# A down product in fp16 terms in place of fp32r: three fp16 copies of each weight tile, scaled by a bound from norms

## The chip, the core and the metric

The kernel runs on one core of one Trainium2 chip. Its time is device microseconds of one execution, the median of several. The engines have short names in the profile: PE is the matrix engine (TensorE) and PEld its weight load, DVE is VectorE, ACT is ScalarE, POOL is GpSimd, and SP issues the DMAs.

## What is computed

The input x has 2048 rows of 576. Two branches read it and are mixed row by row by a gate g:

```python
g = _sigmoid((x * gate_w).sum(-1, keepdims=True))
a = _A_ref(x, A_wq, A_wk, A_wv, A_wo, A_beta)   # attention with memory, 32 heads, 4 segments of 512
b = _B_ref(x, B_w_gate, B_w_up, B_w_down)       # (silu(x @ w_gate) * (x @ w_up)) @ w_down
return g * a + (1 - g) * b
```

The change touches the last product of the second branch, with `w_down` of 4608 x 576: the **down product**. All inputs are fp32, and the kernel keeps nearly fp32's precision by splitting each operand into a high and a low term and adding three products: high by high, high by low, low by high.

## The kernel before, in words

**Stages.** Up to 235 us of the profile the kernel projects x to q, k, v and updates the memory, segment by segment (`qk`, `v_step`, `mem_step`). In between it takes sums of squares or greatest squares of x and of the first weights (`square` on ACT, `peak` on DVE) into columns of a small tile `sc`, 128 columns of one fp32 per partition. From them come powers of two as scales: `sx` for x, `sw[i]` for the weights of four tiles f (i = f // 4); `power` sums a column across partitions by a matmul with ones (L141) and rounds by integer operations on the bits (L142 to L146); `back` makes the inverse `iw[i]` (L149, L150).

**The feed-forward loop** goes over 2 halves of the rows (1024 each) and 36 tiles f of 128 hidden columns. For one f, seven products of a fast scheme (`seven`, a function called with j = 0 to 6; each is seven f16 matmuls of 512 columns, six on L1304 and the last on L1307) make gate and up sums in three PSUM banks `a`, `y`, `xx`, with copies on ACT and additions on DVE between them (L1381, L1384, L1388, L1391, L1395, L1396). Two Silus (L1398, L1400, each with the scale `iw`) and two products on DVE (L1406, L1407) give `sg0` and `sg1`, the hidden rows. ACT copies them into `hh` and DVE subtracts to get `hl`, both fp32r: `split_by` (L1188, L1189) one or two steps later, or `split` (L124, L125) in the third f of a chunk.

**Chunks and steps.** Three f's make a chunk (CH = 3; q = f % 3 is 0, 1, 2). When the next chunk starts, its first f carries the down product of the chunk before: 16 **groups** (8 blocks of 128 rows by 2 column halves of 320 and 256 of the 576), each of 9 matmuls (3 f's by 3 terms) into one bank (`down_part`, L1089), and `down_end` adds the bank to `ya` on DVE (L1098; L1096 copies for the first chunk). Each f has eight steps (`tick`, k = 0 to 7), called between the products. `beat` in a step first runs what `defer(n, ...)` queued for it n steps ago, then groups (SHARE gives 2, 2, 3, 3, 3, 3 for steps 2 to 7 of the first f) and steps of the attention (`att`). In the first half attention steps run only in steps that have groups; in the second half also elsewhere. So the order on each engine is fixed by the program, and each engine runs its own list in that order. Attention contributes matmuls on L846, L957, L985, L987, exponentials on ACT (L961), maxima on DVE (L864), casts on DVE (L1056) and subtractions on POOL (L1058), in three rotating banks (`ts_tile`).

**Weights, first half only.** `w_make` makes f16 operands of gate and up for the next f: sums on POOL (L318), high parts on ACT (L322), low parts on DVE (L326), stored for the second half, which loads them (`w_fetch`). `d_load` brings a tile of `w_down` (L266), `d_split` makes its high part on ACT (L1070, scaled by `iw`) and the low part on DVE (L1071), and the pair, `dw`, is stored to `dc` (L1072); the second half loads it back (`d_fetch`, L1077). `glance` loads weights and squares them on ACT (L132) in the first f of seven chunks, for `sw[i]` of i = 2 to 8; the sum, `power` and `back` follow in the second f. At f = 24, 27, 30 and 33 `x_second` makes the second half's operands of x (L1232, L1239, L1242). Between the halves, the last chunk's 16 groups run without products beside them. In the tail the output projection (L172) runs with the second half's last 16 groups.

## Time and profile before

| | us |
|---|---|
| median of 3 runs | 1751.36 (1747.77 to 1753.06) |
| profiled execution | 1750.37 |
| its span in the profile | 1748.7 |
| projections, to the first feed-forward product | 0 to 235 |
| first half, f = 0 to 35 | 235 to 910 |
| second half with the groups between the halves | 910 to 1657 |
| tail | 1657 to 1749 |

A group line of the profile reads: line, engine, operation, output and inputs by name, shape and count, then busy time, mean ns of one, then the engine's idle time before them and who ended it. In a timeline the columns are start, length, engine, line, operation; consecutive equal instructions are merged into one row with a count. In the view of one line or tile the three numbers are shortest, median and longest ns. In the view by windows each engine has its busy time and its number of instructions. Matmuls overlap in time, so the length of one is not what it costs.

### The profile page before, as it was taken

The page shows a single profiled execution, that of the slowest core. Times are in us where ns is not written, and L with a number is a line of the kernel's source. Part 1 is how long each engine was busy: PE and PEld are TensorE (multiplying, and loading weights), DVE is VectorE, ACT ScalarE, POOL GpSimd, SP SyncE. Part 2 cuts the span into 40 slices and gives each one's busy share as a digit, 9 for nine tenths or more (in the row PEclk, how much of TensorE's full clock was granted, in tenths as well). Part 3 has the DMA queues.
Part 4 walks back from the last instruction along what each step waited for, and adds up shares of the span by engine and source line. Part 5 has one row for each costly group of instructions (what it writes and reads, how often), then busy time and mean ns, then how long its engine had stood idle before and what let it go on. Part 6 is the DMA issues. An engine that isn't in the chain of part 4 may idle for free.

```text
span 1748.7 us, 34878 instructions
## 1 busy us (share of the span) xinstructions
PE 1714.6 (98%) x12241; PEld 1217.6 (70%) x12241; DVE 1326.4 (76%) x3239; ACT 1024.4 (59%) x1800; POOL 841.7 (48%) x1065
## 2 busy tenths in 40 slices
PE   9999999999999999999999999999999999999999
PEld 7889856666766676567656757766756766776699
DVE  6677676788878888888886877778778777775455
ACT  6756575767676666655754565566456466455411
POOL 3325552255545554665542764555546565553121
PEclk9999999999999999999999999999999999999999
DMA  8656776776687666545554477587577569654544
GB/s 284 224 211 225 237 244 206 224 234 191 179 247 225 205 186 193 185 142 153 169 165 150 123 181 182 132 207 170 125 185 196 143 147 210 167 125 129 184 137 139
DMA packets 341667, 321.89 MB, mean 184 GB/s; under 512 B 193396, under 2 KB 258676, under 8 KB 341492
## 3 DMA queue, kind: packets, MB, share of 16 engines
q1 hardware_dynamic: 341492, 319.67, 63.1%
q8 instruction: 96, 1.57, 0.4%
q14 instruction: 79, 0.65, 0.1%
HBM read 188.51 MB, written 104.86 MB: 168 GB/s over the span
## 4 chain that ended last, share of the span: by engine, by line
PE 79%; DVE 7%; ACT 5%; DMA 3%; issue 3%; SPq 2%; POOL 1%; DVEq 0%; ACTq 0%; POOLq 0%
PE bank L1304 33%; PE bank L1089 23%; PE bank L172 7%; PE bank L1307 5%; PE bank L846 4%; PE bank L957 2%; PE bank L985 2%; PE bank L987 1%; DMA stw<-q 1%; PE bank L919 1%; ACT L1297 1%; DVE xo L1242 1%; PE bank L460 1%; ACT L1398 1%; DMA wo__21835<-wc 0%
## 5 line engine op out<-in xcount | busy, mean ns | idle before, releaser
L1089 PE MATMUL bank<-dw,hh 128*128 128x320 f32 (+1 forms) x2304 | 510.0, 314 | 9.2 <-DVE ya L1098 7.0
L1089 PEld LDWEIGHTS bank<-dw,hh 128*128 128x128 f32 x2304 | 380.3, 190 | 35.0 <-DVE ya L1098 11.1
L1089 PE MATMUL bank<-dw,hl 128*128 128x320 f32 (+1 forms) x1152 | 341.0, 296 | 0.6 <-DVE hl L125 0.5
L1058 POOL TENSOR_TENSOR p<-pe,p 128x512 f16<-128x512 f32 x220 | 273.5, 1243 | 88.1 <-DVE p L1056 60.6
L961 ACT ACTIVATE pe<-bank 128x512 f32<-128x512 f32 x220 | 130.8, 594 | 222.3 <-PE bank L957 197.6
L1098 DVE TENSOR_TENSOR ya<-bank,ya 128x320 f32<-128x320 f32 x352 | 157.5, 453 | 90.1 <-PE bank L1089 87.2
L1089 PEld LDWEIGHTS bank<-dw,hl 128*128 128x128 f32 x1152 | 218.4, 190 | 1.1 <-DVE hl L125 1.1
L1307 PE MATMUL bank<-xr,rh 128*128 128x512 f16 x504 | 191.0, 379 | 0.0
L969 POOL TENSOR_SCALAR_AFFINE_SELECT pe<-pe 128x256 f32<-128x256 f32 (+1 forms) x220 | 92.4, 420 | 188.5 <-ACT pe L961 184.6
L864 DVE CUSTOM_DVE_ANT_0 junk<-bank,cm 128x128 bf16<-128x128 f32 (+2 forms) x352 | 169.8, 483 | 15.0 <-PE bank L846 10.0
L318 POOL TENSOR_TENSOR ws<-raw 128x256 f32<-128x256 f32 x72 | 67.5, 938 | 153.2 <-DMA raw<-in_wf_dram 91.3
L846 PE MATMUL bank<-kst,qst 108*128 108x512 bf16 (+3 forms) x512 | 125.2, 300 | 5.4 <-ACT pe L961 2.1
L1189 DVE TENSOR_TENSOR hl<-row,hh 128x512 fp32r<-128x512 f32 x120 | 110.9, 924 | 16.3 <-ACT hh L1188 16.1
L1056 DVE CAST p<-pe 128x512 f16<-128x512 f32 x220 | 108.2, 492 | 0.1
L1391 ACT ACTIVATE row<-bank 128x512 f32<-128x512 f32 x72 | 43.1, 598 | 106.8 <-PE bank L1307 106.6
L957 PE MATMUL bank<-qst,kst 111*128 111x512 bf16 (+3 forms) x352 | 104.2, 303 | 0.0
L1396 DVE TENSOR_TENSOR row<-bank,row 128x512 f32<-128x512 f32 x72 | 49.7, 691 | 70.7 <-ACT bank L1395 70.3
L172 PE MATMUL bank<-xo,qhi 128*128 128x512 f32 x288 | 91.9, 399 | 0.6 <-DVE xo L125 0.5
L1307 PEld LDWEIGHTS <-rh 128*128 128x128 f16 x504 | 49.3, 98 | 59.5
L1395 ACT ACTIVATE bank<-bank 128x512 f32<-128x512 f32 x72 | 41.9, 582 | 83.1 <-PE bank L1307 81.2
L416 POOL TENSOR_TENSOR q<-qr,q 128x512 bf16<-128x512 f32 x36 | 47.1, 1308 | 82.7 <-ACT q L415 70.2
L903 POOL TENSOR_TENSOR xo<-xr,xo 128x512 f16<-128x512 f32 x60 | 71.0, 1184 | 21.7 <-DVE xo L902 12.4
(1067 smaller groups left out, 4121.8 us busy)
## 6 DMA issues: line engine op xcount, KB each, us to landing
xo<-in_wf_dram SPq DMA_DIRECT2D x65, 320.0 KB
dc<-dw SPq DMA_DIRECT2D x36, 576.0 KB
dw<-dc SPq DMA_DIRECT2D x36, 576.0 KB
raw<-in_wf_dram SPq DMA_DIRECT2D x72, 256.0 KB
rh<-rc SPq DMA_DIRECT2D x72, 168.0 KB
draw<-in_wd_dram SPq DMA_DIRECT2D x36, 288.0 KB
xo<-in_xT_dram SPq DMA_DIRECT2D x33, 256.0 KB
vd<-vps SPq DMA_DIRECT2D x8, 912.0 KB
```

Of the source, the lines that this page charges most:

```text
L172: nc.tensor.matmul(t, st[n], mv[n], start=(n == 0), stop=(n == 13))
L846: nc.tensor.matmul(t[:, c:c + w], qs[:KR, pr, P * i:P * i + P], ks[:KR, pr, 0:w], start=True, stop=True)
L864: nc.vector.tensor_tensor_reduce(junk.bitcast(BF)[:, :w], t[:, c:c + w], cm[:, L - w:L], 1.0, -3.0e38, OP.add, OP.max, m[:, k:k + 1])
L957: nc.tensor.matmul(t[:, c:c + w], ks[:KR + 3, pr, P * j:P * j + P], qs[:KR + 3, pr, P * j:L], start=True, stop=True)
L961: nc.scalar.activation(pe, t, AF.Exp, scale=SCALE)
L1056: nc.vector.tensor_copy(p1, pe)
L1058: nc.gpsimd.tensor_sub(p2, pe, p1)
L1089: nc.tensor.matmul(t, p, q[:, cs], start=(f == CH * c and n == 0), stop=(f == CH * c + CH - 1 and n == 2))
L1098: nc.vector.tensor_add(ya[:, i, cs], t, ya[:, i, cs])
L1189: defer(k + 1, lambda: nc.vector.tensor_sub(lo, src, f32(hi)))
L1304: nc.tensor.matmul(t, w[:, p, z], x[z][:, q], start=first and n == 0, stop=False, skip_group_check=True)
L1307: nc.tensor.matmul(t, rem[:, RPOS[j]], XR[j], start=False, stop=True, skip_group_check=True)
```

## The change

The down product's operands become fp16.

- **Weights.** `dw` holds three fp16 copies instead of two fp32r: the high part, the low part, and the high part divided by 2^11 (STEP). The first two are scaled by a column made in `d_scale`; the third is one more DVE operation. The store to `dc` comes a step later and moves 432 KB for 576.
- **Hidden rows.** The two products on DVE take a third factor, the column `hk[i]`; `hh` is 2^-11 of the result in fp16, `hl` the rest at full size (2^11 larger), so the third product is `hl` by the third copy. Both are half as large in memory.
- **Scales.** `weigh(i)` takes the place of the sum, `power` and `back`: one sum across partitions of the 8 or 9 columns, then 17 (19 for i < 2) small DVE operations that also give `hk`, `ha`, `hb`. `reach` makes a bound of x in the projections, and two squares there move from ACT to DVE. `d_look` squares each weight tile on ACT with a sum; `d_scale` turns three such sums into one scale per chunk, with one or two multiplications on POOL.
- **Places.** All three loads of a chunk's `w_down` stand in steps 0, 1, 2 of its first f (three buffers), the looks in steps 4, 5, 6, `d_scale` in step 0 of the second f; the splits stay where they were. `weigh` stands in step 2 of the third f, where the sum stood in step 1 and the rest in steps 5 and 6 of the second.
- **Results.** `down_end` multiplies the bank by the column `inv[c]` as it adds it to `ya`.

The core of the diff:

```diff
+FLOOR = 1e-10
+STEP = 2.0 ** 11
...
-    dc = dram.tile([FT, P, 2 * D], F32, name="dc")
+    dc = dram.tile([FT, P, 3 * D], F16, name="dc")
...
     sc = consts.tile([P, 128], F32, name="sc")
-    junk = consts.tile([P, L], F16, name="junk")
-    one, sx = sc[:, ONE:ONE + 1], sc[:, SX:SX + 1]
+    junk = consts.tile([P, D], F16, name="junk")
+
+    def column(k):
+        return sc[:, k:k + 1]
+
+    one, sx, xq = column(ONE), column(SX), column(19)
+    hk, ha, hb = ([column(20 + 9 * i + j) for i in range(FT // 4)] for j in range(3))
+    inv = [column(23 + 9 * c) for c in range(9)] + [column(16 + c) for c in range(3)]
     sw = [sc[:, SW + i:SW + i + 1] for i in range(FT // 4)]
...
     def peak(src, c, dst=None):
-        nc.vector.tensor_tensor_reduce(src if dst is None else dst, src, src, 1.0, 0.0, OP.mult, OP.max, sc[:, c:c + 1])
+        nc.vector.tensor_tensor_reduce(src if dst is None else dst[:, :src.shape[1]], src, src, 1.0, 0.0, OP.mult, OP.max, sc[:, c:c + 1])
 
...
 
-    def power(out, t):
-        nc.tensor.matmul(t, one.to_broadcast([P, P]), out, start=True, stop=True)
-        nc.vector.tensor_scalar_max(out, t, 1e-24)
+    def grade(out, t, low=FLOOR):
+        nc.vector.tensor_scalar_max(out, t, low)
         bits = out.bitcast(I32)
...
         nc.vector.tensor_single_scalar(bits, bits, 23, OP.logical_shift_left)
+
+    def across(t, src):
+        nc.tensor.matmul(t, one.to_broadcast([P, P]), src, start=True, stop=True)
+
+    def power(out, t):
+        across(t, out)
+        grade(out, t)
         nc.vector.tensor_scalar_mul(out, out, TOP)
 
-    def back(i):
+    def reach(t):
+        across(t, sc[:, 0:4 * NT])
+        nc.vector.tensor_reduce(sc[:, 0:4], t.rearrange("p (s k) -> p s k", k=NT), axis=AX.X, op=OP.add)
+        nc.vector.tensor_reduce(xq, sc[:, 0:4], axis=AX.X, op=OP.max)
+        nc.vector.tensor_scalar(xq, xq, sx, sx, op0=OP.mult, op1=OP.mult)
+        nc.vector.tensor_mul(xq, xq, xq)
+
+    def weigh(i, t):
+        c = 20 + 9 * i
+        n = 9 if i < 2 else 8
+        e, z, m = sc[:, 0:8], column(8), sc[:, 9:13]
+        across(t[:, :n], sc[:, c:c + n])
+        nc.vector.tensor_reduce(sw[i], t[:, :n], axis=AX.X, op=OP.add)
+        grade(sw[i], sw[i])
+        nc.vector.tensor_scalar_mul(sw[i], sw[i], TOP)
+        nc.vector.tensor_scalar(e, t[:, 0:8], sw[i], sw[i], op0=OP.mult, op1=OP.mult)
+        if i < 2:
+            nc.vector.tensor_scalar(z, t[:, 8:9], sw[i], sw[i], op0=OP.mult, op1=OP.mult)
+            nc.vector.tensor_scalar_add(e, e, z)
+        v = e.rearrange("p (f u) -> p f u", u=2)
+        nc.vector.tensor_mul(m, v[:, :, 0], v[:, :, 1])
+        nc.vector.tensor_reduce(z, m, axis=AX.X, op=OP.max)
+        nc.vector.tensor_mul(z, z, xq)
+        grade(z, z, 2.0 ** 26)
         nc.vector.tensor_mul(iw[i], sw[i], sx)
+        nc.vector.tensor_scalar(hk[i], z, 4.0 * STEP * TOP, iw[i], op0=OP.mult, op1=OP.mult)
+        nc.vector.tensor_scalar(ha[i], hk[i], iw[i], 1.0 / STEP, op0=OP.mult, op1=OP.mult)
+        nc.vector.reciprocal(hb[i], ha[i])
         nc.vector.reciprocal(iw[i], iw[i])
...
     def d_load(f):
-        r = fp.tile([P, D], F32, name="draw", bufs=2)
+        r = fp.tile([P, D], F32, name="draw", bufs=3)
         nc.sync.dma_start(r, wd[f])
...
             z = GAUGE.get(t, ())
-            return [lambda m=m, fn=(square if k == 2 else peak): gauge(m, fn) for k, m in enumerate(z)]
+            return [lambda m=m, fn=(square if k == 2 and m > 9 else peak): gauge(m, fn) for k, m in enumerate(z)]
 
...
                 if s == 2:
-                    if n == 4:
-                        mid.append(lambda: total(sw[1], 29, 38))
                     if n == 6:
-                        mid.append(lambda: power(sw[1], lone_tile([P, 1])))
-                        mid.append(lambda: back(1))
+                        mid.append(lambda: weigh(1, lone_tile([P, 9])))
                     if n == 0:
...
                         power(sx, lone_tile([P, 1]))
-                    if n == 2:
-                        total(sw[0], 20, 29)
+                    if n == 4:
+                        reach(lone_tile([P, 4 * NT]))
                     if n == 6:
-                        power(sw[0], lone_tile([P, 1]))
-                        back(0)
+                        weigh(0, lone_tile([P, 9]))
                 if s:
...
         def d_tile():
-            return fp.tile([P, 2, D], F32R, name="dw")
+            return fp.tile([P, 3, D], F16, name="dw")
+
+        def d_look(f):
+            nc.scalar.activation(junk, draw[f], AF.Square, accum_out=column(123 + f % CH))
+
+        def d_scale(c):
+            t, r = ts_tile([P, CH]), sc[:, 13:16]
+            across(t, sc[:, 123:126])
+            grade(r, t)
+            nc.vector.tensor_scalar_mul(r, r, TOP)
+            fs = range(CH * c, CH * c + CH)
+            at = sorted({f // 4 for f in fs})
+            for i in at:
+                z = [f % CH for f in fs if f // 4 == i]
+                z = r[:, z[0]:z[-1] + 1]
+                nc.vector.tensor_scalar(z, z, ha[i], 2.0 ** 100, op0=OP.mult, op1=OP.min)
+            nc.vector.tensor_reduce(inv[c], r, axis=AX.X, op=OP.min)
+            for n, i in enumerate(at):
+                nc.gpsimd.tensor_mul(column(121 + n), inv[c], hb[i])
+            nc.vector.reciprocal(inv[c], inv[c])
 
...
             d = d_tile()
-            k = iw[f // 4]
+            k = column(121 + f // 4 - f // CH * CH // 4)
             defer(1, lambda: nc.scalar.activation(d[:, 0], r, AF.Copy, scale=k))
-            defer(2, lambda: nc.vector.scalar_tensor_tensor(d[:, 1], r, k, f32(d[:, 0]), op0=OP.mult, op1=OP.subtract))
-            defer(3, lambda: nc.sync.dma_start(dc[f], f32(d).rearrange("p a n -> p (a n)")))
+            defer(2, lambda: nc.vector.scalar_tensor_tensor(d[:, 1], r, k, d[:, 0], op0=OP.mult, op1=OP.subtract))
+            defer(3, lambda: nc.vector.tensor_scalar_mul(d[:, 2], d[:, 0], 1.0 / STEP))
+            defer(4, lambda: nc.sync.dma_start(dc[f], d.rearrange("p a n -> p (a n)")))
             return d
...
             d = d_tile()
-            nc.sync.dma_start(f32(d).rearrange("p a n -> p (a n)"), dc[f])
+            nc.sync.dma_start(d.rearrange("p a n -> p (a n)"), dc[f])
             return d
...
                 d = ws[half, f]
-                dh, dl = d[:, 0], d[:, 1]
-                for n, (p, q) in enumerate(((hh, dh), (hh, dl), (hl, dh))):
-                    nc.tensor.matmul(t, p, q[:, cs], start=(f == CH * c and n == 0), stop=(f == CH * c + CH - 1 and n == 2))
+                for n, (p, q) in enumerate(((hh, 0), (hh, 1), (hl, 2))):
+                    nc.tensor.matmul(t, p, d[:, q, cs], start=(f == CH * c and n == 0), stop=(f == CH * c + CH - 1 and n == 2))
 
...
             if c == 0:
-                nc.vector.tensor_copy(ya[:, i, cs], t)
+                nc.vector.tensor_scalar_mul(ya[:, i, cs], t, inv[c])
             else:
-                nc.vector.tensor_add(ya[:, i, cs], t, ya[:, i, cs])
+                nc.vector.scalar_tensor_tensor(ya[:, i, cs], t, inv[c], ya[:, i, cs], op0=OP.mult, op1=OP.add)
             if c == FT // CH - 1 and hf and half == 0:
...
 
-        def split_by(k, hi, lo, src):
-            defer(k, lambda: nc.scalar.activation(hi, src, AF.Copy))
-            defer(k + 1, lambda: nc.vector.tensor_sub(lo, src, f32(hi)))
+        def h_high(hi, src):
+            nc.scalar.activation(hi, src, AF.Copy, scale=1.0 / STEP)
+
+        def h_low(hi, lo, src):
+            nc.vector.scalar_tensor_tensor(lo, hi, -STEP, src, op0=OP.mult, op1=OP.add)
+
+        def split_by(k, hi, lo, src, lag=1):
+            defer(k, lambda: h_high(hi, src))
+            defer(k + lag, lambda: h_low(hi, lo, src))
 
...
                 plan += [z for z in looked if z[0] >= 0]
-            if half == 0 and pos % 3 == 1 and 2 <= i < FT // 4:
-                plan += [(1, lambda i=i: total(sw[i], 20 + 9 * i, 28 + 9 * i)),
-                         (5, lambda i=i: power(sw[i], ts_tile([P, 1]))), (6, lambda i=i: back(i))]
+            if half == 0 and pos % 3 == 2 and 2 <= i < FT // 4:
+                plan.append((2, lambda i=i: weigh(i, ts_tile([P, 8]))))
             if pos == 24:
...
                 if half == 0:
-                    if (q, k) in ((0, 1), (1, 0), (1, 5)):
-                        g = f + (q == 1 and k == 5)
-                        draw[g] = d_load(g)
+                    if q == 0 and k < CH:
+                        draw[f + k] = d_load(f + k)
+                    if q == 0 and 4 <= k < 4 + CH:
+                        d_look(f + k - 4)
+                    if q == 1 and k == 0:
+                        d_scale(f // CH)
                     if (q, k) in ((1, 1), (1, 7), (2, 5)):
...
             ops, rem = wops.pop((half, f)), rhs[f % 2]
-            hh = fp.tile([P, 2, L], F32R, name="hh")
-            hl = fp.tile([P, 2, L], F32R, name="hl")
+            hh = fp.tile([P, 2, L], F16, name="hh")
+            hl = fp.tile([P, 2, L], F16, name="hl")
             hs[half, f] = hh, hl
...
             seven(xx, 6, False)
-            nc.vector.tensor_mul(sg0, xx, sg0)
-            nc.vector.tensor_mul(sg1, p5, sg1)
-            if q == CH - 1:
-                defer(2, lambda t=(hh[:, 0], hl[:, 0], sg0): split(*t))
-            else:
-                split_by(2, hh[:, 0], hl[:, 0], sg0)
+            nc.vector.scalar_tensor_tensor(sg0, xx, hk[f // 4], sg0, op0=OP.mult, op1=OP.mult)
+            nc.vector.scalar_tensor_tensor(sg1, p5, hk[f // 4], sg1, op0=OP.mult, op1=OP.mult)
+            split_by(2, hh[:, 0], hl[:, 0], sg0, int(q < CH - 1))
             split_by(3, hh[:, 1], hl[:, 1], sg1)
```

## The prediction

> **What bounds the kernel now.** I read the page first, then stages, then single steps. The page gives the span and the engines' shares. The greatest group, two thirds of the down product (L1089), follows.
>
> ```profile
> span 1748.7 us, 34878 instructions
> PE 1714.6 (98%) x12241; PEld 1217.6 (70%) x12241; DVE 1326.4 (76%) x3239; ACT 1024.4 (59%) x1800; POOL 841.7 (48%) x1065
> L1089 PE MATMUL bank<-dw,hh 128*128 128x320 f32 (+1 forms) x2304 | 510.0, 314 | 9.2 <-DVE ya L1098 7.0
> ```
>
> TensorE is busy 98% and idles 9 us before 2304 down matmuls. A busy mean (314 ns) is a latency, so it prices nothing; spacing of starts does. By stage (projections; first half; second half; tail), then L1089 alone in the last three stages:
>
> ```profile
> 0.00:235.00 235.00, 223.75 (x1293) 196.61 (x1294) 170.25 (x400) 150.02 (x302) 103.53 (x119) 0.99 0.69 231
> 235.00:910.00 675.00, 663.78 (x4412) 433.95 (x4410) 555.68 (x1236) 446.98 (x779) 334.33 (x421) 1.00 0.64 197
> 910.00:1657.00 747.00, 739.01 (x5868) 499.51 (x5867) 548.51 (x1505) 413.96 (x687) 384.91 (x502) 1.00 0.64 163
> ...
> 235.00:910.00 675.00, 253.46 (x1586) 223.22 (x1587) 1.00 0.64 197
> 910.00:1657.00 747.00, 270.40 (x1728) 242.65 (x1726) 1.00 0.64 163
> 1657.00:1749.00 92.00, 21.40 (x144) 19.74 (x144) 1.00 0.42 139
> ```
>
> Columns are length, then PE, PEld, DVE, ACT, POOL busy, clock (1.00: full), DMA. VectorE is 82% busy in the first half, 73% in the second. One chunk of the first half (f = 15, 16, 17; the cuts are the starts of each f's last L1307), then one with x_second (24 to 26):
>
> ```profile
> 495.80:528.20 32.40, 32.16 (x273) 24.81 (x272) 25.89 (x70) 22.06 (x42) 16.18 (x25) 1.00 0.70 206
> 528.20:543.30 15.10, 15.10 (x86) 9.09 (x85) 14.35 (x32) 9.82 (x18) 11.85 (x14) 1.00 0.50 124
> 543.30:553.90 10.60, 10.60 (x51) 4.83 (x50) 8.34 (x14) 8.73 (x16) 3.33 (x4) 1.00 0.96 339
> ...
> 670.10:703.20 33.10, 32.60 (x275) 24.96 (x273) 28.65 (x72) 18.99 (x31) 18.48 (x24) 1.00 0.59 172
> 703.20:719.10 15.90, 15.16 (x84) 8.82 (x83) 14.62 (x26) 8.35 (x15) 11.97 (x13) 1.00 0.44 137
> 719.10:729.70 10.60, 10.60 (x50) 4.77 (x49) 8.42 (x12) 8.68 (x16) 4.32 (x4) 1.00 0.81 262
> ```
>
> So TensorE sets the pace, but in the second f of a chunk VectorE has 0.75 us free of 15.10. The change relieves the first and loads the second: that decides the forecast.
>
> **The matmuls.** Starts of every third matmul of one down group (320 columns, then 256), then two L1307 with seven f16 matmuls of 512 columns from one to the other:
>
> ```profile
> 518.24 0.31 PE L1089 MATMUL bank<-dw,hl 128*128 128x320 f32 x1
> 518.68 0.31 PE L1089 MATMUL bank<-dw,hl 128*128 128x320 f32 x1
> ...
> 519.50 0.28 PE L1089 MATMUL bank<-dw,hl 128*128 128x256 f32 x1
> 519.86 0.28 PE L1089 MATMUL bank<-dw,hl 128*128 128x256 f32 x1
> ...
> 497.27 0.38 PE L1307 MATMUL bank<-xr,rh 128*128 128x512 f16 x1
> 498.78 0.38 PE L1307 MATMUL bank<-xr,rh 128*128 128x512 f16 x1
> ```
>
> f32: 0.44/3 = 147 ns at 320, 0.36/3 = 120 at 256. f16: 1.51/7 = 216 at 512; by proportion 135 at 320 and 108 at 256. A 256-column bf16 matmul and the start of the next bound this from the other side:
>
> ```profile
> 526.47 0.28 PE L957 MATMUL bank<-qst,kst 111*128 111x256 bf16 x1
> 526.59 0.38 PE L846 MATMUL bank<-kst,qst 108*128 108x512 bf16 x1
> ```
>
> It takes 0.12 us, no less than f32, though at a change of rows (111 to 108). I take 136 and 110, near the proportion, whose matmuls have the same 128 x 128 weights: 1728 x 11 ns + 1728 x 10 ns = **36.3 us** saved (ends: 12 ns each, 41; 320 alone, 19). By window: 16.6 in the first half, 18.1 in the second with its opening groups, 1.5 in the tail. The count of matmuls is unchanged.
>
> The Trainium skill (TensorE: Matmul & The Clock Gate, Back-to-back issue gap) gives N/2.4 + 2.5 ns with no term for the type: 215.8 at 512, as the trace has it, but 135.8 at 320, where the f32 rows show 147. By the rule f32 would already run at f16's pace and nothing would be saved; the rows speak against it.
>
> **VectorE's added work.** Rows of a scalar-by-column operation and of a plain one of equal size, both with one input in PSUM; then the small operations on sc:
>
> ```profile
> L1466 DVE SCALAR_TENSOR_TENSOR ya<-bank,gg,ya x16: 517/518/520, 1714.4 to 1745.3; 128x288 f32<-128x288 f32 x16
> L436 DVE TENSOR_TENSOR r<-bank,vps x32: 442/455/459, 41.7 to 237.1; 128x288 f32<-128x288 f32 x32
> ...
> 542.50 0.15 DVE L142 TENSOR_SCALAR sc<-bank 128x1 f32<-128x1 f32 x1
> 542.68 0.15 DVE L144 TENSOR_SCALAR sc<-sc 128x1 int32<-128x1 int32 x1
> ...
> L1056 DVE CAST p<-pe x220: 382/422/1371, 348.2 to 1608.4; 128x512 f16<-128x512 f32 x110
> ```
>
> A column scalar costs 518 - 455 = 63 ns; a small operation occupies 0.19 us. Per chunk of the first half:
>
> - 16 group ends (down_end) x 63 ns = 1.0 us; 6 products with hk = 0.4. The lower halves (h_low) keep size and a constant scalar: 0 (bounds -0.2 and +0.4).
> - the third copy, 3 casts of 576: 0.4 each, near L1056's median (0.2 to 1.4), 1.2 us.
> - d_scale: 3 in grade, TOP, one or two scalings, minimum, reciprocal: 7.5 x 0.19 = 1.4 us, plus a wait, since the reciprocal overwrites what POOL's multiplication reads.
> - weigh: 17 small operations in the third f for 7 in the second: +1.9 in the seven chunks from f = 3 to 23.
>
> That is 5.9 us with weigh, 4.0 without, against 58.1 - 48.6 = 9.5 and 59.6 - 51.7 = 7.9 free, while the chunk loses 144 x 10.5 ns = 1.5 us. VectorE comes to some 96%: nothing overflows as a sum, but places do. Second f: 14.35 + 1.4 + 0.8 + 0.3 - 1.3 = 15.6 of 14.8 left. Third: 8.34 + 3.2 + 0.5 = 12.0 of 10.6. So about 2.2 us are late when the next chunk opens. There stands:
>
> ```profile
> 498.82 0.61 ACT L124 ACTIVATE hh<-row 128x512 fp32r<-128x512 f32 x1
> 499.46 0.69 DVE L125 TENSOR_TENSOR hl<-row,hh 128x512 fp32r<-128x512 f32 x1 [1.14 <-ACT hh L124]
> 500.32 0.49 PE L1089 MATMUL bank<-dw,hh 128*128 128x320 f32 x1
> ```
>
> hl ends at 500.15, TensorE starts the group at 500.3, and 1.1 us of the delay is taken up by the wait for ACT: the first group is 1.1 to 1.2 us late, seven times, 8 us. Without weigh (four chunks) the second f alone overruns by 14.62 + 2.5 - 15.6 = 1.5; half of it is slack before the next f's first product, which needs L1396 to have read its bank: 0.7 x 4 = 3 us. Together **11 us** (0 to 35: 0 if TensorE's slack of some three products at each point absorbs it, 35 if every late us lands on TensorE in 11 chunks, with POOL's queue added). POOL's queue: d_scale's multiplication stands behind L1058, and VectorE's reciprocal, the splits and L1388 behind it:
>
> ```profile
> 534.62 1.50 POOL L1058 TENSOR_TENSOR p<-pe,p 128x512 f16<-128x512 f32 x1
> ```
>
> It ends at 536.12, just when d_scale would get there (534.5 + 1.4): half a us, inside those 35.
>
> The Trainium skill (VectorE: DVE Perf Modes, The TRN2 errata) has (N + 151)/0.96 ns for a tensor_tensor in fp32: 457 at 288, as L436; a column scalar isn't in it. If L1466 cost the same, 1.4 us a chunk less would be added; its row says 518.
>
> **ScalarE's added work.** d_look squares 576 columns at steps 4, 5, 6 of the first f. At step 5 ACT is already what TensorE waits for:
>
> ```profile
> 518.17 1.28 ACT L1297 ACT_TABLE_LOAD   x1
> 519.58 0.72 ACT L132 ACTIVATE xo<-xo 128x640 f32<-128x640 f32 x1
> 520.30 0.57 ACT L961 ACTIVATE pe<-bank 128x512 f32<-128x512 f32 x1
> 520.93 0.27 PE L846 MATMUL bank<-kst,qst 108*128 108x256 bf16 x1 [0.24 <-ACT pe L961]
> ```
>
> L132 holds ACT 0.72 us for 640, so 0.66 for 576, ahead of the exponential; TensorE also arrives 0.3 us earlier, after three shorter groups. One us more wait in the seven chunks that have L132 there: **7 us** (0 to 7). Elsewhere ACT has over 10 us free in the first f. No square brings a table load: none stands at L132.
>
> **The rest.** The stage of f = 0 to 2, and a sum across partitions:
>
> ```profile
> 235.00:268.00 33.00, 31.34 (x145) 13.93 (x143) 24.67 (x44) 25.67 (x46) 14.52 (x18) 1.00 0.84 287
> ...
> 541.87 0.28 PE L141 MATMUL bank<-sc 128*128 128x1 f32 x2
> 542.01 0.38 PE L1304 MATMUL bank<-xo,wo__6647 128*128 128x512 f16 x1
> ```
>
> In f = 0 to 2 no group runs and ACT is busy 25.7 of 33 us; three looks wait for loads that have just been issued: 2 us (0 to 5). 21 sums across partitions for 10, 0.14 us each on TensorE: 1.5 us. Second half and projections: VectorE has 198 us free of the second half's 747 and gets 1.4 in each of twelve chunks; two squares go to it and two weigh in the projections: 2 us (0 to 5). SP: loads move from the second f into the first, and each copy is 432 KB instead of 576: 0, hidden by TensorE; uncovered it would be a late landing for w_make, about a us.
>
> Sum: -36.3 + 11 + 7 + 2 + 1.5 + 2 = -12.8. The profiled execution took 1750.4 us, 1.0 under the median 1751.4; so 1737.6 or 1738.6: **1738**. The second half keeps nearly all, the first nothing.
>
> **Rivals.**
> 1. Everything added hides: VectorE's lateness meets slack and ACT's look fills idle time. For it: TensorE hardly waits now, and three f16 products (4.5 us) lie between L1388's place and the product that needs it. Against: 0.15 us of slack at hl. Then 36.3 less 2 to 12: 1714 to 1728, say 1720. Chance 0.19.
> 2. It doesn't do what it says: f16 at 256 columns is as slow as f32, as L957's 0.12. Saving 19, costs 23.5: 1755, within 0.3%. So too if the costs come out half as large again (1749). Chance 0.17.
> 3. Slower: VectorE becomes the bound of the first half. Mechanism: its small chains (d_scale, weigh) stand in line before L1388, L1396 and hl, each of which holds a TensorE product, and POOL holds the reciprocal. If 35 us and more land on TensorE instead of 11, at over 3 us in each of 11 chunks, time passes before's: 35 + 5 for contention between VectorE and POOL gives 1738 + 29 = 1767. From 1.2 us a chunk more than I take the gain is gone, from 1.7 it is slower. Chance 0.19; the skill's rule with no saving at all (1774) has 0.02 of it.
>
> **How the numbers follow.** Forecast 0.45, between 1728 and 1746. About 0.3% (5 us) is what a measurement of this kernel can tell from no change. Faster: 0.45 + 0.19 = 0.64; same: 0.17; slower: 0.19. Range 1716 to 1764: it leaves out a tenth on either side.
>
> **What would show it.** Spacing of L1089's successors 136 and 110 ns. Second-half chunks 1.3 to 1.5 us shorter, first-half chunks equal. Waits of PE for hl, for the bank that L1396 reads, and for the exponential, larger. VectorE over 90% busy from f = 9 to 35. Wrong it would be if spacing stays at 147 and 120, if first-half chunks shrink like the others (rival 1), or if they grow by over 2 us (rival 3).

## The result, and the profile after

The changed kernel takes **1774.46 us** (median of 4 runs, 1773.73 to 1776.07) beside 1749.66 us for the kernel before on the same chip (1747.77 to 1753.06): a ratio of 1.0141, 95% interval 1.0121 to 1.0161. It is 1.4% slower, where 1738 was forecast. The page of its profiled execution (1776.07 us), the span, the engines and the first group of the down product:

```profile
span 1774.4 us, 35271 instructions
PE 1688.2 (95%) x12267; PEld 1094.0 (62%) x12267; DVE 1392.2 (78%) x3467; ACT 1047.0 (59%) x1868; POOL 839.5 (47%) x1083
L1144 PE MATMUL bank<-dw,hh 128*128 128x320 f16 (+1 forms) x2304 | 436.9, 286 | 25.9 <-DVE ya L1153 21.3
```

TensorE is busy 26 us less than before and the span is 26 us longer. The lines have moved: L1089 is now L1144, L1098 (group end) L1153, L1388 (the y sum) L1451, L1304 L1365, L961 (exponential) L997. By stage, cut at the same events as before (first feed-forward product, end of f = 35, end of the second half):

```profile
0.00:239.40 239.40, 225.91 (x1293) 196.84 (x1294) 177.73 (x432) 148.62 (x296) 104.28 (x119) 0.99 0.67 227
239.40:954.20 714.80, 655.30 (x4434) 378.52 (x4435) 596.35 (x1430) 471.08 (x852) 333.33 (x439) 1.00 0.58 179
954.20:1683.90 729.70, 720.34 (x5869) 436.38 (x5868) 565.06 (x1506) 413.89 (x688) 383.25 (x502) 1.00 0.64 159
1683.90:1774.40 90.50, 86.65 (x674) 82.26 (x672) 53.10 (x100) 13.39 (x34) 18.68 (x24) 1.00 0.43 142
```

Before, these stages took 234.7, 674.9, 747.4 and 91.7 us. So the second half and the tail gave what was forecast (-17.7 and -1.2; forecast -18.1 and -1.5, with 1 to 2 back). The projections lost 4.7, and the **first half lost 39.9**, where the forecast's terms add up to about 5 (21.5 of costs less 16.6 saved). The spacing of the matmuls is not to blame. Starts of matmuls six apart, 320 columns and then 256:

```profile
541.09 0.30 PE L1144 MATMUL bank<-dw,hl 128*128 128x320 f16 x1
...
541.90 0.30 PE L1144 MATMUL bank<-dw,hl 128*128 128x320 f16 x1
...
542.26 0.27 PE L1144 MATMUL bank<-dw,hl 128*128 128x256 f16 x1
...
542.91 0.27 PE L1144 MATMUL bank<-dw,hl 128*128 128x256 f16 x1
```

0.81/6 = 135 ns and 0.65/6 = 108: the forecast's 136 and 110. The chunk f = 15, 16, 17, whose f's took 32.40, 15.10 and 10.60 us before:

```profile
518.90:551.70 32.80, 31.06 (x273) 20.53 (x272) 25.96 (x72) 23.41 (x47) 16.10 (x25) 1.00 0.76 235
551.70:568.40 16.70, 14.98 (x86) 8.16 (x85) 15.95 (x36) 9.68 (x18) 11.83 (x16) 1.00 0.44 117
568.40:580.50 12.10, 11.09 (x53) 4.97 (x52) 10.53 (x29) 9.43 (x17) 4.20 (x4) 1.00 0.52 172
```

The second f lost 1.6 us, the third 1.5, the first 0.4. The view of TensorE's waits (who is waited for, us in total, times, longest) in the first half, first of the kernel before, then of the changed one:

```profile
PE bank L1089 <- DVE ya L1098: 6.0, 10, 1.4
PE bank L846 <- ACT pe L961: 1.4, 6, 0.3
...
PE bank L1304 <- DVE bank L1388: 0.8, 2, 0.5
```

```profile
PE bank L1144 <- DVE ya L1153: 19.1, 20, 2.1
PE bank L1365 <- DVE bank L1451: 18.8, 22, 1.7
PE bank L882 <- ACT pe L997: 10.2, 10, 1.2
PE bank L155 <- ACT junk L1104: 4.5, 1, 4.5
```

Four waits grew by 44 us: for the group ends, for the y sum, for the exponential behind the looks, and once for a look. The second is nearly new (0.8 us before). VectorE's row in step 0 to 2 of f = 16 (start, length, line), and beside it TensorE's:

```profile
557.16 0.84 DVE L1092 CAST p<-pe 128x512 f16<-128x512 f32 x1
557.92 0.15 DVE L149 TENSOR_SCALAR sc<-bank 128x3 f32<-128x3 f32 x1
558.10 0.17 DVE L151 TENSOR_SCALAR sc<-sc 128x3 int32<-128x3 int32 x1
558.31 1.02 DVE L152 TENSOR_SCALAR sc<-sc 128x3 int32<-128x3 int32 x1
...
560.56 0.16 DVE L1120 RECIPROCAL sc<-sc 128x1 f32<-128x1 f32 x1 [0.45 <-POOL sc L1119]
560.76 0.92 DVE L322 SCALAR_TENSOR_TENSOR rt<-rr,sc,rt 128x448 f16<-128x448 f32 x1
561.60 1.21 DVE L366 SCALAR_TENSOR_TENSOR wo__6695<-ws,sc,wo__6695 128x512 f16<-128x512 f32 x1
562.74 0.68 DVE L1246 SCALAR_TENSOR_TENSOR hl<-hh,row 128x512 f16<-128x512 f16 x1
563.34 0.69 DVE L1451 TENSOR_TENSOR bank<-bank,row 128x512 f32<-128x512 f32 x1
```

```profile
561.98 0.38 PE L1368 MATMUL bank<-xr,rh 128*128 128x512 f16 x1
564.08 1.46 PE L1365 MATMUL bank<-xo,wo__6695 128*128 128x512 f16 x6 [1.72 <-DVE bank L1451]
```

The scale of the chunk (L149 to L1120) occupies VectorE from 557.92 to 560.72, 2.8 us. Behind it, in line, stands the y sum, `y = a + p5`, which reads bank `a`. The product that TensorE wants to start at 562.2, `seven(a, 4, False)`, adds to that bank, so it waits until the sum has read it.

### The profile page after: what moved, and what is told of

It is laid out like the page before. It is cut to its first block, busy times and chain, and to the rows that moved or that the text cites. A ratio compares the mean times of both kernels' runs of the same rounds, so it can differ in the third digit from the quotient of the medians.

```text
span 1774.4 us, 35271 instructions
## 1 busy us (share of the span) xinstructions
PE 1688.2 (95%) x12267; PEld 1094.0 (62%) x12267; DVE 1392.2 (78%) x3467; ACT 1047.0 (59%) x1868; POOL 839.5 (47%) x1083
## 4 chain that ended last, share of the span: by engine, by line
PE 55%; DVE 18%; ACT 10%; issue 9%; DMA 5%; POOL 3%; SPq 1%; DVEq 0%; ACTq 0%; POOLq 0%
PE bank L1365 20%; PE bank L1144 16%; PE bank L212 7%; PE bank L1368 3%; PE bank L882 3%; PE bank L993 2%; DVE ya L1153 2%; ACT L1461 2%; DVE junk L900 2%; DVE hl L1246 1%; DMA rc<-rt 1%; PE bank L1021 1%; ACT row L1463 1%; ACT L1358 1%; DVE p L1092 1%
## 5 line engine op out<-in xcount | busy, mean ns | idle before, releaser
L1144 PE MATMUL bank<-dw,hh 128*128 128x320 f16 (+1 forms) x2304 | 436.9, 286 | 25.9 <-DVE ya L1153 21.3
L1144 PE MATMUL bank<-dw,hl 128*128 128x320 f16 (+1 forms) x1152 | 329.9, 286 | 1.1 <-DVE hl L1246 1.1
L1144 PEld LDWEIGHTS <-hh 128*128 128x128 f16 x2304 | 224.5, 98 | 117.1 <-issue 31.3
L997 ACT ACTIVATE pe<-bank 128x512 f32<-128x512 f32 x220 | 130.1, 591 | 194.4 <-PE bank L993 183.0
L1153 DVE SCALAR_TENSOR_TENSOR ya<-bank,sc,ya 128x320 f32<-128x320 f32 x352 | 176.0, 511 | 60.9 <-PE bank L1144 58.5
L1246 DVE SCALAR_TENSOR_TENSOR hl<-hh,row 128x512 f16<-128x512 f16 x144 | 124.1, 862 | 27.1 <-ACT hh L1243 27.0
L358 POOL TENSOR_TENSOR ws<-raw 128x256 f32<-128x256 f32 x72 | 66.3, 921 | 152.0 <-DMA raw<-in_wf_dram 104.5
L1144 PEld LDWEIGHTS <-hl 128*128 128x128 f16 x1152 | 112.5, 98 | 30.8 <-DVE hl L1246 1.8
L1454 ACT ACTIVATE row<-bank 128x512 f32<-128x512 f32 x72 | 43.0, 597 | 103.8 <-PE bank L1368 103.8
L1243 ACT ACTIVATE hh<-row 128x512 f16<-128x512 f32 x144 | 89.1, 619 | 5.0 <-DVE row L1469 4.1
L1469 DVE SCALAR_TENSOR_TENSOR row<-bank,sc,row 128x512 f32<-128x512 f32 x72 | 53.8, 748 | 42.4 <-ACT row L1461 20.5
```

Of the source, the lines that this page charges most:

```text
L997: nc.scalar.activation(pe, t, AF.Exp, scale=SCALE)
L1144: nc.tensor.matmul(t, p, d[:, q, cs], start=(f == CH * c and n == 0), stop=(f == CH * c + CH - 1 and n == 2))
L1153: nc.vector.scalar_tensor_tensor(ya[:, i, cs], t, inv[c], ya[:, i, cs], op0=OP.mult, op1=OP.add)
L1246: nc.vector.scalar_tensor_tensor(lo, hi, -STEP, src, op0=OP.mult, op1=OP.add)
```

## The experiments

Each time is the median of its runs, the ratio that to the kernel before on the same chip (medians 1749.0 to 1749.8), with its 95% interval. Theory A: a small operation costs what it delays, that is, its **place** ahead of a release counts. Theory B: VectorE is full, so each of its us costs alike (**load**).

**1. Without the scale of a chunk.** The call of `d_scale` is taken out; the looks stay.

```diff
-                    if q == 1 and k == 0:
-                        d_scale(f // CH)
```

> The changed kernel without d_scale: its sum across partitions, its seven or eight small operations on VectorE and the one or two on POOL are left out (the weight copies are scaled by 1 and the results by columns that hold other numbers); the looks on ACT stay. Theory A (place): the small operations stand ahead of L1451, whose read of bank a holds TensorE's very next product but one, so they cost the second f of each chunk nearly all of its lengthening (22.1 us over 12 chunks, 6.7 of them in f = 1). Expected 1774 - 18 = 1756, and the waits of PE for L1451 down from 18.8 us to about 9 (those in the third f stay). Theory B (load): VectorE is simply full in the first half, and each us of work counts alike; d_scale is 1.4 of 5.9 us added per chunk, so a quarter of the 40 us lost there: 1764.

Measured: 1752.51 us, 1.0018 (1.0008 to 1.0027). The scale costs 22 us, more than either theory gave (18 and 10): in the profiled executions the second f's are 18.0 us shorter, and the waits for the y sum fell from 18.8 to 2.6 us. The exponential still waits 10.2.

**2. The old chain for the weights' scale** instead of `weigh` for i = 2 to 8, at its old steps in the second f.

```diff
-            if half == 0 and pos % 3 == 2 and 2 <= i < FT // 4:
-                plan.append((2, lambda i=i: weigh(i, ts_tile([P, 8]))))
+            if half == 0 and pos % 3 == 1 and 2 <= i < FT // 4:
+                plan += [(1, lambda i=i: total(sw[i], 20 + 9 * i, 28 + 9 * i)),
+                         (5, lambda i=i: power(sw[i], ts_tile([P, 1]))), (6, lambda i=i: back(i))]
```

> The changed kernel with the sum, power and the inverse of before for i = 2 to 8, seven small operations at their old steps in the second f, in place of weigh's 17 in the third (hk, ha and hb of i = 1 serve all). Theory A (place): the third f loses its 1.2 to 1.5 us in seven chunks, about 9 us, and the old operations come back behind L1451, where they cost little: 1765. Theory B (load): 1.9 of 5.9 us per chunk in seven chunks, a third of 25 us: 1766. It sizes weigh; it does not tell the theories apart by the time, but by the third f: A has it back at 10.6 us, B has the second f longer by what the third gains.

Measured: 1769.37 us, 1.0111 (1.0096 to 1.0126). Third f's gave 6.4 us back, first f's 3.5, second f's took 1.7 more. In all 5.1 us, little over half of the 9 expected; the third f's of the seven chunks came down from between 11.6 and 12.1 us to between 10.8 and 11.3, not to the 10.6 of A, so this run does not decide between the two.

**3. Group ends without a factor** (a plain copy or sum).

```diff
-                nc.vector.scalar_tensor_tensor(ya[:, i, cs], t, inv[c], ya[:, i, cs], op0=OP.mult, op1=OP.add)
+                nc.vector.tensor_add(ya[:, i, cs], t, ya[:, i, cs])
```

> The changed kernel with the plain copy and addition of before at the ends of groups, without the factor inv (the result is left unscaled): 384 operations on VectorE some 63 ns shorter, 24 us of busy time. Theory A (place): ends of groups are off the path except where TensorE waits for ya (21 us in the changed kernel, 7 before): about 6 us back, 1768. Theory B (load): 1.0 of 5.9 us per chunk, and the same in the second half where nothing was lost: 7 us, 1767. A third reading, that the longer ends are what holds the first f, would give back over 14 us: 1760.

Measured: 1772.93 us, 1.0133 (1.0117 to 1.0148). 384 ends of 60 ns, 23 us of VectorE, were worth 1.5, which the noise does not tell from nothing: A had put 6 on it and B 7, so both look too high, and the third reading (14) falls.

**4. The same work, the scale three steps later**, behind the y sum.

```diff
-                    if q == 1 and k == 0:
+                    if q == 1 and k == 3:
                         d_scale(f // CH)
-                    if (q, k) in ((1, 1), (1, 7), (2, 5)):
-                        g = f - 1 if k == 1 else f
+                    if (q, k) in ((1, 3), (1, 7), (2, 5)):
+                        g = f - 1 if k == 3 else f
```

> The changed kernel with the same work in another place: d_scale stands in step 3 of the second f, behind L1451, in place of step 0, and the first split stands in step 3 in place of step 1. Theory A (place): the wait for L1451 in the second f goes, some 10 us; part of it comes back at L1459, which the next f's first product needs: 1774 - 10 = 1764 (1758 to 1769), and waits of PE for L1451 at 9 us. Theory B (load): VectorE does the same work, so the time stays at 1774 within 3.

Measured: **1764.61 us**, 1.0088 (1.0073 to 1.0104), as A had it. The second f's gave back 17.3 us, the third took 5.2. In the view of waits of this kernel:

```profile
PE bank L1365 <- DVE bank L1451: 4.5, 12, 0.8
```

Same operations, same count, 18.8 us of waits down to 4.5: place, not load, for this part.

**5. Without scale and looks.**

```diff
-                    if q == 0 and 4 <= k < 4 + CH:
-                        d_look(f + k - 4)
```

> The kernel after, without the scale of each chunk (the sum across partitions and the VectorE and GpSimd operations behind it, as in the run with the looks alone) and now also without the three Squares of the raw down weights on ScalarE; the factors of the down weights are 1.0 throughout, so the output is not the reference's. It differs from the run with the looks alone (1752.5 us) by the looks only. Theory A (place): the looks stand in steps 4 to 6 of a chunk's first f ahead of the silus and the exponential of step 5, for which TensorE waited 1.1 to 1.2 us in nine first f's (10.9 us together), and in f = 1 TensorE's products waited for ScalarE, about 5 us: 1752.5 - 9 - 5 = 1738 us. Rival (the looks only fill gaps of ScalarE, and the exponential is late for the sake of the silus and the table load): 1751 us.

Measured: 1742.15 us, 0.9952 (0.9936 to 0.9969); 10.4 less than run 1, where the place theory had 14 and its rival 1.5. The waits for the exponential fell from 10.2 to 4.0 us, f = 1 from 17.1 to 11.7. Part of the exponential's wait stays.

**6. The looks in other steps**, on top of run 4.

```diff
-                    if q == 0 and 4 <= k < 4 + CH:
-                        d_look(f + k - 4)
+        LOOK = ((0, 6), (0, 7), (1, 0))
...
+                    if (q, k) in LOOK:
+                        d_look(f - q + LOOK.index((q, k)))
```

> The whole work of the kernel after, with the scale of a chunk at step 3 of its second f behind the y sum (as in the run that gave 1764.6 us), and the three looks at steps 6 and 7 of the first f and step 0 of the second instead of steps 4, 5 and 6 of the first. Theory A (place): the exponential of step 5 waits no longer (10 us back), and in the first chunk the looks wait less for raw rows that have only just been asked for (2 us of some 4): 1764.6 - 12 = 1753 us, with the waits for the exponential under 3 us. Theory B (load: ScalarE is full in the first f's, and a look costs the same wherever it stands): 1764 us, the wait moved to the exponential or the copies of the next steps.

Measured: 1754.4 us, 1.0032 (1.0022 to 1.0041): 10.2 less than run 4 with the same work, so place again. The exponential, in this kernel:

```profile
PE bank L882 <- ACT pe L997: 4.0, 8, 0.5
```

That is the 4.0 of the run without looks: in these steps three squares a chunk add nothing to this wait.

**7. `weigh` one step later** on top of run 6, and **8. the third copy on GpSimd** on top of that.

```diff
-                plan.append((2, lambda i=i: weigh(i, ts_tile([P, 8]))))
+                plan.append((3, lambda i=i: weigh(i, ts_tile([P, 8]))))
...
-            defer(3, lambda: nc.vector.tensor_scalar_mul(d[:, 2], d[:, 0], 1.0 / STEP))
+            defer(3, lambda: nc.gpsimd.tensor_scalar_mul(d[:, 2], d[:, 0], 1.0 / STEP))
```

> The run with the looks at steps 6, 7 and 0 and the late scale, and beside it the chain of small VectorE operations that makes the bound of four f's (in the third f of seven chunks) one step later, so that it stands behind the y sum of step 2 instead of ahead of it. Theory A (place): the waits for the y sum in the third f (0.4 to 0.7 us each) and part of those for the weights' low half (0.5 us) go: 4 to 8 us less than its twin, so 1747 us if that gives 1753. Theory B (load): within 1.5 us of its twin.

> The kernel of the run before (late scale, late looks, chain of the bound one step later), with the third copy of the down weights (128x576 f16, 0.48 us on VectorE, 36 times, 17 us) made by GpSimd instead. Theory B (load: VectorE sets the pace of the first half): 8 us or more less than its twin, 1739 if that gives 1747. Theory A (place): the copy stands behind the releases of the products' banks in its step, so 3 us or less are given back, 1744 to 1747; and a little may be lost, since a VectorE operation beside a GpSimd one took 0.5 to 1 us longer in the scale's chain.

Measured: 1752.66 us, 1.0018 (1.0009 to 1.0027), and 1749.68, 1.0006 (0.9997 to 1.0015). The first gave 1.7 of the 4 to 8 that A expected, next to B's 1.5 and not clear of the noise: in the profiled executions the third f's are 4.1 us shorter and the first f's 6.5 longer, but these are the fastest execution of run 6 and the slowest of run 7. The second gave 3.0, on A's side: 17 us of VectorE's busy time were worth 3.

**9 to 11. What is left when all small chains go.** Run 9 has no scale, no look and, instead of `weigh` and `reach`, the old chains at their old places, in the projections too. Run 10 has plain group ends besides; run 11 also the third copy on GpSimd and the two products of each f without `hk`.

```diff
-            nc.vector.scalar_tensor_tensor(sg0, xx, hk[f // 4], sg0, op0=OP.mult, op1=OP.mult)
+            nc.vector.tensor_mul(sg0, xx, sg0)
```

> The kernel after without any of its small chains: no looks, no scale of a chunk, no bound (the scale of the projections' weights is made by the few operations and in the places of the kernel before), all factors of the down product constants, so the output is not the reference's. What is left of the change: f16 matmuls, group ends and products with a factor, the third copy. Against the run without looks (1742 us) the bound's chain goes from the third f's (0.7 us in each of ten) and from the projections (5 us): 1730 us. Theory C (in a chunk's first f the time that TensorE saves is handed back, because VectorE and ScalarE set the pace there; the run without looks still had 8.3 us of waits in five first f's, where the kernel before had 2.0): the first f's stay at 32 to 33 us and the sum is 1730. The first rival of the prediction (nothing but the chains ever cost anything): 1720 to 1723 us, first f's at 31.3.

> The run with no chains, and beside it group ends without a factor (a plain copy or sum, 450 instead of 510 ns, 384 of them). If it is VectorE's length of these ends that holds the first f's (theory C with VectorE as the pace): 28 ends a chunk less 60 ns, 1.2 to 1.7 us in each of nine, so 1717 to 1720 us where its twin gives 1730. If the waits for the ends come from elsewhere (the exponentials of ScalarE, or the order in which the steps are issued): within 2 us of its twin.

> The run with no chains and plain ends, and beside it the third copy on GpSimd and the two products of each f without a factor (each 60 to 120 ns shorter): VectorE then has no more work than in the kernel before, and less in the low halves. If VectorE sets the pace of the first f's: they fall by a further 0.5 us each and the second f's stay, some 5 us less than its twin, 1713 to 1715 us. If it does not: within 2 us of its twin, and what holds the first f's is ScalarE or the order of issue.

Measured: 1729.38 us, 0.9886 (0.9872 to 0.9901); 1728.41, 0.9874 (0.9860 to 0.9889); **1721.91**, 0.9837 (0.9821 to 0.9853). In run 9 the first f's fell to 31.6 to 32.3 us in f = 9 to 21 (32.5 to 33.4 before). That lies between theory C (32 to 33) and the prediction's first rival (31.3); the time is the 1730 of C. Run 10 says once more that the ends' length is worth some 1 us at most; run 11 that the third copy on VectorE and the longer products of each f are worth 6.5 us, half of the 13 to 15 that VectorE as the pace would have given. The first half of run 11, then its chunk f = 15 to 17:

```profile
237.00:902.20 665.20, 645.18 (x4409) 375.93 (x4410) 549.50 (x1235) 446.70 (x780) 401.45 (x456) 1.00 0.62 192
...
493.90:525.40 31.50, 30.97 (x274) 20.60 (x273) 24.84 (x70) 22.10 (x42) 17.89 (x26) 1.00 0.76 232
525.40:540.20 14.80, 14.80 (x86) 8.18 (x85) 14.13 (x31) 9.80 (x18) 14.64 (x15) 1.00 0.42 101
540.20:550.70 10.50, 10.50 (x50) 4.74 (x49) 9.35 (x15) 8.62 (x16) 5.86 (x6) 1.00 0.82 279
```

The chunk is 1.3 us shorter than before (56.8 for 58.1), nearly the 1.5 of the forecast: this is what the f16 products are worth when nothing stands in their way.

**12. Everything kept, the bound in three pieces**: sums at step 3 of the third f, the rest (L201 to L207 here) at steps 5 and 6 of the next first f; the chains of the first eight f's out of the projections into f = 0 and f = 2.

```diff
+                plan.append((3, lambda i=i: weigh_one(i, ts_tile([P, 8]))))
+            if half == 0 and pos % 3 == 0 and 3 <= i <= FT // 4:
+                plan += [(5, lambda i=i - 1: weigh_two(i)), (6, lambda i=i - 1: weigh_three(i))]
```

> The whole work of the kernel after, put elsewhere: the scale of a chunk and its looks later, the bound's chain in three pieces (sums and squares at step 3 of the third f, the rest at steps 5 and 6 of the next first f), for the first eight f's out of the projections into f = 0 and f = 2, and the third copy on GpSimd. Theory A (place): the projections give back 5 us, the third f's 0.3 us each: 1749.7 - 5 - 3 = 1742 us, 0.4 per cent faster than the kernel before. Theory B (load): the pieces cost in the first f's and in f = 0 what they cost before, 1748 to 1750 us.

Measured: 1751.85 us, 1.0018 (1.0009 to 1.0028): 2 more than run 8. The projections gave back 3.5, the first f's took 9.1. VectorE and TensorE in f = 12:

```profile
473.94 1.12 DVE L201 TENSOR_TENSOR sc<-sc 128x1 f32<-128x1 f32 x1
...
475.73 0.53 DVE L1174 SCALAR_TENSOR_TENSOR ya<-bank,sc,ya 128x320 f32<-128x320 f32 x1
```

```profile
476.31 0.43 PE L1165 MATMUL bank<-dw,hh 128*128 128x320 f16 x2 [1.63 <-DVE ya L1174]
```

The pieces stood ahead of another release: a group end, and TensorE's next group needs its bank.

**13. Part of the bound on GpSimd**, on top of run 8: five operations less in VectorE's row, its reciprocals three steps later. **14** has besides the chains of the first eight f's and of the first chunk moved.

```diff
+        nc.gpsimd.tensor_mul(k, sw[i], sx)
...
+        nc.gpsimd.tensor_scalar(hk[i], z, 4.0 * STEP * TOP, k, op0=OP.mult, op1=OP.mult)
+        nc.gpsimd.tensor_scalar(ha[i], hk[i], k, 1.0 / STEP, op0=OP.mult, op1=OP.mult)
```

> The whole work of the kernel after, as in the run with the third copy on GpSimd (1749.7 us), but with fewer small VectorE operations in the bound's chain: the product with the scale of x, the two factors behind it and no more stand on GpSimd, one maximum is folded into the product before it, and the two reciprocals come three steps later. VectorE keeps 13 operations in each of seven third f's where it had 17 to 18 in one row. Theory B for what is left (every small operation on VectorE costs about its 0.19 us, wherever it stands): 4 to 5 operations less in seven f's and in the projections, 6 to 8 us, 1743 us. Theory A (only the operations ahead of a release that TensorE waits for cost anything, and these stood behind them already): within 2 us of its twin, 1748 to 1750.

> As the run before with the bound on GpSimd in part, and beside it the chains for the first eight f's out of the projections (into f = 0 and f = 2, where VectorE had 3 us and 1 us to spare), and in the first chunk the raw down weights loaded at steps 5 to 7 of f = 0, looked at in steps 3 to 5 of f = 1, scaled at step 7. The projections gave back 3.5 us when these chains were taken out of them before, f = 0 took 0.8 of it, and f = 1 waited 1.3 us for its small weights behind the raw down weights: 3 to 4 us less than its twin, so 1739 to 1741 us if the twin gives 1743, and 1745 if the twin gives 1749. Rival (the time moves to the next f's): the twin's time.

Measured: 1764.53 us, 1.0086 (1.0070 to 1.0101), and 1764.16, 1.0082 (1.0066 to 1.0098): run 13 missed both theories by 15 us and more, and run 14 came out at its twin's time, as its rival had it. The third f's did not change (11.3 us in f = 17, with or without the five operations). In the profiled executions of runs 8 and 13 the next first f's took 14.6 us more and the projections 3.0. GpSimd, ScalarE and TensorE from the end of f = 11 into f = 12 of run 13 (L365 is L358, L369 is L362, L1454 is L1444 in the changed kernel):

```profile
450.56 1.39 POOL L192 TENSOR_SCALAR sc<-sc 128x1 f32<-128x1 f32 x1
451.91 0.72 POOL L365 TENSOR_TENSOR ws<-raw 128x256 f32<-128x256 f32 x1
452.60 1.24 POOL L365 TENSOR_TENSOR ws<-raw,ws 128x256 f32<-128x256 f32 x1
```

```profile
453.87 0.72 ACT L369 ACTIVATE wo__5325<-ws,sc 128x512 f16<-128x512 f32 x1 [2.12 <-POOL ws L365]
454.61 1.28 ACT L1367 ACT_TABLE_LOAD   x1
...
456.01 0.58 ACT L1454 ACTIVATE bank<-bank 128x512 f32<-128x512 f32 x1
```

```profile
456.64 0.59 PE L1374 MATMUL bank<-xo,wo__5287 128*128 128x512 f16 x2 [2.00 <-ACT bank L1454]
```

GpSimd makes the sum of a weight late, ScalarE's copy of it waits 2.1 us, behind it in line stand a table load and the copy that TensorE needs: 2.0 us of wait on TensorE. Over the first half:

```profile
PE bank L1374 <- ACT bank L1454: 16.5, 9, 2.1
```

That is 13.7 us more than such waits take in run 8. They cost more than themselves: in f = 12, 15, 18, 21 and 24 TensorE's granted clock is about half for some 3.4 us behind the wait, where run 8's first half has no such stretch.

```profile
458.00:461.00 3.00, 3.00 (x12) 1.63 (x11) 1.92 (x3) 1.97 (x6) 1.42 (x4) 0.50 1.04 282
```

At half speed 3.4 us lose 1.7, so the five come to some 8 us (an estimate from these figures); these five first f's are 2.2 to 3.0 us longer than in run 8, f = 6 and f = 9, which have the wait and not the slow clock, 0.4 and 1.3. Other waits are shorter than in run 8, so the parts add up to more than the 15 us. An engine that nothing seemed to depend on has places too.

**15 and 16. Only the chains of the first eight f's moved**, on top of run 8 (on VectorE, in f = 0 and f = 2), and the first chunk's loads and looks later besides.

```diff
+            if pos == 0:
+                plan += [(0, lambda: reach(ts_tile([P, 4 * NT]))), (3, lambda: weigh_one(0, ts_tile([P, 9]))),
+                         (4, lambda: weigh_two(0)), (5, lambda: weigh_three(0))]
```

> The whole work of the kernel after: as the run with the third copy on GpSimd (1749.7 us), with only the chains for the first eight f's taken out of the projections, in three pieces in f = 0 and f = 2 on VectorE, and the bound of the later f's in one piece in the third f's as there. Place: the projections give back 3.5 us, f = 0 and f = 2 take 0.9, f = 3 perhaps 0.8: 1747 to 1748 us. If instead the pieces of the spread run cost wherever they stood: 1749 to 1752.

> As the run before, and in the first chunk the raw down weights loaded at steps 5 to 7 of f = 0, looked at in steps 3 to 5 of f = 1 and scaled at its step 7. In the run that had this beside the GpSimd chains, f = 1 was 1.8 us shorter, and f = 2 and f = 3 6.3 us longer. If that was the GpSimd chain of f = 2: 1.5 us less than its twin, 1745 to 1746, the fastest whole version so far and within 0.3 per cent of the kernel before. If it was the later splits: 3 to 5 us more than its twin, 1751.

Measured: 1746.03 us, 0.9991 (0.9979 to 1.0004), and 1749.88, 1.0003 (0.9991 to 1.0014). The first is a little below the 1747 to 1748 of its place theory, the second is on the side of the later splits. Run 15 is the best that has all of the work; it is 28 us faster than the changed kernel and **cannot be told from the kernel before**.

## Why the prediction was wrong

One ladder, each step a difference of two medians, one order of several:

| from the kernel before, 1749 | us | forecast |
|---|---|---|
| f16 matmuls, half-precision hidden rows (run 11) | -27 | -36 |
| third copy on VectorE instead of GpSimd, products with `hk` (run 11 to 10) | +6.5 | part of the 11 |
| group ends with a factor (10 to 9) | +1 | part of the 11 |
| bound `weigh` and `reach`, projections too (9 to 5) | +12.8 | part of the 11, and 2 |
| looks (5 to 1) | +10.4 | 7 + 2 |
| scale of a chunk (1 to the change) | +22 | part of the 11, and the 1.5 of the sums |
| sum (+24.8 by the two medians on one chip) | +25.7 | -12.8 |

- **The matmuls**: right in the spacing, and in the second half and tail. Run 11 has -9.7 us in the first half where 16.6 was forecast, -17.6 in the second, -1.4 in the tail, and +2.3 in the projections. For the first half's missing 7 us the shares are: f = 1 0.9 longer, f = 6 to 8 1.0 short, and f = 24 to 35 gaining 1.7 where four chunks would give 6. There the waits for group ends, kernel before and then run 11, have grown by as much as is missing:

```profile
PE bank L1089 <- DVE ya L1098: 5.5, 9, 1.4
PE bank L1155 <- DVE ya L1164: 10.0, 11, 1.9
```

  TensorE is done sooner and waits longer; the forecast put nothing for this. The Trainium skill (TensorE: Matmul & The Clock Gate, Back-to-back issue gap) has a gap of N/2.4 + 2.5 ns, which gives 135.8 and 109.2 ns at 320 and 256 columns; the f16 rows agree (135, 108), the f32 rows of before (147, 120) do not. By the rows 12 ns for each of the second half's 1728 matmuls would be 20.7 us, by the forecast's 11 and 10 it was 18.1; it gained 17.6.
- **The lateness of VectorE: the step that failed.** The prediction had 11 us, 8 for `hl` at the chunk's start and 3 for L1396, and put nothing for L1388; under rival 1 it says that "three f16 products (4.5 us) lie between L1388's place and the product that needs it". To the product that uses the sum, `seven(y, 5)`, it is two by the program. And the sum also reads bank `a`, to which the next product but one adds: only `seven(xx, 3)`, 1.5 us, lies between. The scale's row, for which 1.4 us and a wait had been added up, took 2.8. So the scale, ahead of L1388 by its place, arrived on TensorE in nearly every chunk, 18.8 us of waits at L1451, while `hl` cost 1.1. By kind of f the first half lost 6.4 us in the first f's, 22.1 in the second (6.7 of them in f = 1) and 11.3 in the third: the lateness did not gather until the next chunk's `hl`, as the prediction had it, but landed where it arose. Rival 3 had this mechanism and named L1388 among its places; at 40 us for place and contention it gave 1767. The 1774 of the rule that saves nothing is nearer, but by luck: run 11 shows that the saving was there. Rival 3 had a chance of 0.19, beside a sum of busy times that left room (96%). The sum was not what was asked: VectorE was busy 85.5% of f = 9 to 35, where over 90% was to be the sign, run 4 has the same sum and is 10 us faster, runs 3 and 10 take 23 us off it for 1 to 1.5. (Rival 1's 36.3 less 2 to 12 gives 1716 to 1727, not from 1714.)
- **The bound's chain** was added as 1.9 us of work in seven chunks and then counted as part of the lateness at `hl`. Together with the projections it cost 12.8. That its place is the reason is not shown: a step later it gave 1.7 us (run 7), in pieces it cost 2 more (run 12).
- **The looks**: right in the mechanism (they hold the exponential of step 5) and nearly in size.
- **f = 0 to 2**: 7.0 us longer (33.7 to 40.7) for a forecast of 2, bounds 0 to 5. The looks were expected to be late for their loads, but not that TensorE itself would wait for them. The scale begins with a sum across partitions (L155), which stands in TensorE's row and waited 4.5 us in f = 1:

```profile
258.18 0.59 PE L155 MATMUL bank<-sc 128*128 128x3 f32 x2 [4.47 <-ACT junk L1104]
258.63 2.72 PE L1365 MATMUL bank<-xo,wo__2876 128*128 128x512 f16 x6
```

  But that sum is not the cause. Run 1 does not have it, and there the products wait for ScalarE instead, and f = 1 takes 17.1 us (18.0 with it, 11.7 in run 5 without looks):

```profile
256.07 2.48 PE L1365 MATMUL bank<-xo,wo__2876 128*128 128x512 f16 x6 [1.74 <-ACT row L1461]
...
260.15 2.72 PE L1365 MATMUL bank<-xo,wo__2876 128*128 128x512 f16 x6 [1.18 <-ACT bank L1442]
```

  The looks hold up ScalarE's row: the first waits 1.9 us for its load, the others stand ahead of a copy that TensorE needs.

- **Projections and second half**: 4.7 us and none, for 2 (0 to 5).

What stays open: with the chains placed as in run 8, the third f's are still 0.6 us longer than before, also where they have no chain (f = 29, 11.3 for 10.65 us), and the waits that the view names there are 0.2 us; neither the count of small operations (run 13) nor their step (run 7) settles it. In run 11 f = 29 is back at 10.6 us and in run 10 it is not (11.4), which points at the third copy or the products with `hk`; no run parts the two with all else equal. And from f = 24 on the longest wait of TensorE for a group end is 1.4 us or more in every kernel of this study, the one before among them; no run told why.

## What to carry to other kernels

An added operation costs what it delays: follow its engine's row to the next operation that releases something, and count the time from there to whoever reuses that buffer, a product that adds to the bank as well as one that uses the result. Busy time with room to spare says nothing about it, and moving operations only pays when the new place has no such release behind it, on the helper engine too. Before building a cheaper product, price the scaling that it needs: here it ate 27 us of gain, and at its best places just that.
